# Top-32 attention with routed feed-forward: one copy for the values of two units, a third tile's ranks on ScalarE, and a mask half on GpSimd in six more steps

## The chip, the core and the metric

The kernel runs on one core of a Trainium2 chip. The metric is device time in microseconds (us). Before the change it is 788.99 us, the median of three runs (788.96 to 789.6). One further execution was profiled; all views of the trace below are of it.

A core has five engines that matter here: TensorE (PE in the profile, its weight loads PEld), VectorE (DVE), ScalarE (ACT), GpSimd (POOL) and the queue that issues most DMAs (SP). Each works through its own instructions in program order and waits for the others by semaphores.

## The reference, cut to what matters

```python
# q, k, v: (8 batches, 8 heads, 576, 64);  x: (8, 576, 512) = heads side by side
scores = scale * q @ k.T
kth    = the 32nd largest score of each row
attn   = softmax(where(scores >= kth, scores, -1e9))
x      = attn @ v
# routed feed-forward, per batch
gate   = x @ w_gate                        # one number a token, 576 of them
top    = the 128 tokens with the largest gates
out    = x;  out[top] += sigmoid(gate[top]) * (relu(x[top] @ w1) @ w2)
```

Two selections are made: the 32nd largest of every row of scores (36,864 rows of 576), and the 128 largest of 576 gates in each batch. Only where a token stands among the gates is needed, not a full sort: its rank, that is the number of gates greater than its own, is its slot among the 128 chosen.

## The kernel before

**Units and steps.** The work on scores is cut into 144 units, 18 in each of 8 batches. A unit (L1050) is a tile of 128 rows for two heads; the last tile of a batch has only 64 rows, so there a unit holds four heads, in two halves of 64 partitions. The big loop at L1176 makes one step for each unit and is a software pipeline: step n multiplies the scores of unit n+1, and looks after the units n, n-1, n-2, n-3 and n-4 in later stages. In the order of a unit's life:

1. PE multiplies scores into `ps`; ScalarE copies them to `sc` (`keep`, L530).
2. VectorE finds a lower bound for the 32nd largest: 14 MAX8 over seventh parts (`cand`), then some small rounds that end in `bound` (`find_bound`, L544).
3. ScalarE takes the sign of score against bound and counts it (`part`, L578: `sides`, `seen`).
4. GpSimd multiplies scores by signs into `y` (L1148) and appends eight steps (`fill`, L589).
5. VectorE reads the 32nd largest from `y` with two MAX8 (`find_kth`, L598: `next8`).
6. The mask `less` marks scores below it (`mask`, L603). One head's half is made by ScalarE (Relu), the other by GpSimd (`is_lt`).
7. PE transposes scores and adds the mask into `ptr` (`turn`, L642), and once more into the last 128 columns of the bank `av` (`turn_last`, L662). ScalarE takes the exponential of both (`pT`, `last`).
8. PE multiplies by the values into columns 0 to 129 of `av` (`values`, L674): two heads, each with 64 columns and one for the sum of the weights. ScalarE copies them to `xs` (`keep_values`, L706). The bank `av` has one buffer, taken anew in each step (`room_to_turn`, L632).

All instructions of the loop are kept in the order in which they are written; no scheduler moves them. Within a step ScalarE's order is: `pT` of unit n-4, first `sides` of n-1, `last` of n-4, the mask of n-3, what `flush` gives out from the list `late`, copies of transposed keys and queries, `sc` of n+1, what `flush_copies` gives out, second `sides` of n-1, `xs` of n-4. GpSimd's is: mask of n-3, what `flush_pool` gives out from `pool_late`, `y` of n-1. VectorE's is: `cand` and `bound` of n, with other small work put in among the `cand`, then the 32nd largest of n-2.

**The routed part.** When a batch's x is whole, it is stored, and the steps of the next batch carry the batch's feed-forward as a generator (`mixture`, L770). The tables `mix_at` (L1056) say at which steps its pieces are called: with steps numbered 0 to 17 within the next batch, the start is called at 5, tiles 0 to 4 of the gates at 7, 9, 10, 13 and 14, the places at 16, and the expert's matmuls go on into the batch after. The last but one batch has a denser table (L1062). Tile t's piece does this:

- For t of 0 and 1, `weigh_gates` (L823) runs on ScalarE from `late`, in the step after the call: the sign of each gate in the row less this tile's gate, summed, into `sign_sum`. It writes the 576 signs over `pick`, which is rewritten later. After tile 1, both tiles' slots are picked by GpSimd (`choose_slot`, L807) against `slot_signs`, a row of 575 - 2 x slot.
- For t of 2, 3 and 4, `choose` (L845) runs on VectorE from `vector_late`: a comparison of the 576 gates with this tile's, counted into `rank`. GpSimd then picks against `slot`.

`multiply_places` (L941) turns the picks into row numbers on PE. It writes seven columns of the same bank `av`, behind the values (L868), in the step named in `place_steps`; ScalarE copies them out after `xs`. At the end of the feed-forward GpSimd adds the result rows into the output by an indirect DMA (`add_rows`, L989). In six of the steps in which that DMA is issued (`scatter_steps`, L1074; with batches numbered from 0, step 0 of batches 3 to 7 and step 11 of batch 7), `mask_of` at L1240 gives both halves of the mask to ScalarE.

After the loop there is a tail for the last units and the last batch's routed part. It closes with a test whether all results are sure (from L1528); if not, a general loop repeats everything in a slower way.

Of the kernel before, what the change touches and what calls it, by code (L numbers as in the profile page):

```python
# [12 lines left out]
FP32 = mybir.dt.float32  # L13
BF16 = mybir.dt.bfloat16
FP8 = mybir.dt.float8e4
# [17 lines left out]
J = 4  # L33
# [16 lines left out]
def kernel(  # L50
# [12 lines left out]
    P = nc.NUM_PARTITIONS  # L63
    B, H, S, D = q.shape
# [5 lines left out]
    R = S - JP  # L70
    HALF = S // 2
    DE = D + 1
# [47 lines left out]
    for i in range(2):  # L120
# [37 lines left out]
    nc.gpsimd.memset(ranks, 0.0)  # L158


    signs = const.tile([P, B - 1, 2], FP32, name="signs")
    places = const.tile([P, B, 7], FP32, name="places")
    nc.gpsimd.memset(places, 1.0)
    slot_signs = const.tile([P, CAP], FP32, name="slot_signs")
# [1 line left out]
        out=slot_signs,  # L166
# [234 lines left out]
    def bank(pool, name, **how):  # L401
        return pool.tile([P, 512], FP32, name=name, **how)
# [91 lines left out]
    def heads_of(t, g):  # L494

        if t == J:  # L500
            return [[(4 * g + i, 0), (4 * g + 2 + i, R)] for i in range(2)]
        return [[(2 * g + i, 0)] for i in range(2)]
# [97 lines left out]
        for i in range(2):  # L600
            dve.max(next8[:, i, :], y[:, i, :])

    def mask(sc, next8, on=None):  # L603

        less = wkpool.tile([P, 2, S], BF16, name="less")
        for i, engine in enumerate(on or (act, pool)):
            kth = next8[:, i, 7:8]  # L610
            if engine is act:
                act.activation(less[:, i, :], sc[:, i, :], AF.Relu, bias=kth, scale=-1.0)
            else:

                engine.tensor_scalar(
                    out=less[:, i, :],
                    in0=sc[:, i, :],
                    scalar1=kth,
                    scalar2=None,
                    op0=ALU.is_lt,  # L620
                )
        return less
# [6 lines left out]
                tr, less, out_of_reach, start=False, stop=True, skip_group_check=True  # L629
            )  # L630

    def room_to_turn():  # L632
        return ps_tr.tile([P, 2, J, P], FP32, name="ptr"), ps_av.tile(
            [P, 512], FP32, name="av"
        )


    def by_half(a):
# [32 lines left out]
        turn_some(tr, *last)  # L671
        return tr

    def values(t, g, pT, last, av, vs):  # L674

        vt, vpair = vs
        for i, heads in enumerate(heads_of(t, g)):
            for c in range(J):
                for r in (0, R):
                    h = heads[-1 if r else 0][0]
                    pe.matmul(
                        av[r : r + R, i * DE : (i + 1) * DE],
                        by_half(pT)[:, r // R, i * J + c, :],
                        vt[:, h, c, :],  # L690
                        start=(c == 0 and i == 0),
                        stop=False,
                        skip_group_check=True,
                    )
        for r in (0, R):
            h = heads_of(t, g)[0][-1 if r else 0][0]
            pe.matmul(
                av[r : r + R, 0 : 2 * DE],
                last[:, r : r + R],
                vpair[:, h // 2, :, :].rearrange("p h e -> p (h e)"),  # L700
                start=False,
                stop=True,
                skip_group_check=True,
            )

    def keep_values(t, g, av, xs):  # L706
        n = R if t == J else P
        for h, r in heads_of(t, g)[0]:
            act.copy(
                out=xs[0:n, h : h + 2, :].rearrange("p h e -> p (h e)"),  # L710
                in_=av[r : r + n, 0 : 2 * DE],
            )

    def normalise(b, t, xs):
# [55 lines left out]
    def mixture(row0, pg, rank, exact=False, sign_sum=None):  # L770
# [36 lines left out]
        def choose_slot(t, n, slot=slot, rank=None):  # L807
            if rank is None:
                rank = rank_of[:, t : t + 1]
            pool.tensor_scalar(  # L810
                out=pick[0:n, t, :],
                in0=slot[0:n, :],
                scalar1=rank[0:n, :],
                scalar2=None,
                op0=ALU.is_equal,
            )

        for t in range(NT):
            yield
            n = R if t == J else P  # L820


            def weigh_gates(t=t):  # L823
                total = sign_sum[:, t : t + 1]
                act.activation(
                    pick.rearrange("p t c -> p (t c)")[:, 0:S],
                    gate_row,
                    AF.Sign,
                    bias=gate[:, t : t + 1],
                    scale=-1.0,  # L830
                    accum_out=total,
                )
                if t == 1:
                    for u in range(2):
                        pool_late.append(
                            lambda u=u: choose_slot(
                                u, P, slot_signs, sign_sum[:, u : u + 1]
                            )
                        )

            if t < 2 and not exact:
                late.append(weigh_gates)
                continue

            def choose(t=t, n=n):  # L845
                junk = modpool.tile([P, S], FP32, name="junk", tag="scratch")
                dve.tensor_scalar(
                    out=junk[0:n, :],
                    in0=gate_row[0:n, :],
                    scalar1=gate[0:n, t : t + 1],  # L850
                    scalar2=None,
                    op0=ALU.is_gt,
                    op1=ALU.add,
                    accum_out=rank[0:n, t : t + 1],
                )
                if exact:
                    break_ties(t, gate, gate_row, rank)

                pool_late.append(lambda: choose_slot(t, n))

            vector_late.append(choose)
# [3 lines left out]
            ps = ps_misc.tile([P, 512], FP32, name="place_ps", tag="misc")  # L865
        else:
            ps = values_bank[0]
        ps = ps[:, 2 * DE : 2 * DE + 7]  # L868


        done = B if exact else int(row0) // S + 1
# [198 lines left out]
    for b in range(B - 1):  # L1070
        for i in mix_at_of.get(b, mix_at):
            mix_steps.setdefault((b + 1) * per_batch + i, []).append(b)

    scatter_steps = {  # L1074
        (b + 1) * per_batch + mix_at_of.get(b, mix_at)[-1] + 1 for b in range(B - 2)
    }

    place_steps = {}
    for b in range(B - 1):
        n = (b + 1) * per_batch + mix_at_of.get(b, mix_at)[6]  # L1080
# [86 lines left out]
            out=least[:, b : b + 1], in_=kth, axis=mybir.AxisListType.XY, op=ALU.min  # L1167
        )

    def mask_of(n, on=None):  # L1170
        b, i = divmod(n, per_batch)
        masks[n] = mask(scs[n], next8s[b][:, i, :, :], on)
        if i == per_batch - 1 and b < B - 1:
            keep_least(b, bounds.pop(b)[:, :, :, 7], next8s.pop(b)[:, :, :, 7])

    for n in range(-1, N):  # L1176
# [39 lines left out]


        if is_unit(n - 4):
            tr, av = room_to_turn()
            pT, last, exp, turn_rest = weigh(scs.pop(n - 4), tr, av, masks.pop(n - 4))  # L1220
            exp()
        early = is_unit(n - 1) and n + 1 >= NHP
# [14 lines left out]
        if is_unit(n - 4):  # L1237
            turn_rest()()
        if is_unit(n - 3):
            mask_of(n - 3, (act, act) if n in scatter_steps else None)  # L1240
        flush()
        if is_unit(n + 1) and n + 1 >= NHP:
            b, i = divmod(n, per_batch)
# [19 lines left out]
            sign(n - 1, 1)  # L1263
        if is_unit(n - 4):
            b4, t4, g4 = units[n - 4]
            values(t4, g4, pT, last, av, qkv[b4][2])
            if n in place_steps:
                values_bank[0] = av
                next(mixtures[place_steps[n]])
                pieces[place_steps[n]] += 1  # L1270
            if g4 == 0:
                xs = xpool.tile([P, H, DE], FP32, name="xs")
                if t4 == 0:
                    x = xpool.tile([P, NT, HD], FP32, name="x")
                    pg = gates_of[b4 % 2]
                    of_batch[b4] = x, pg
            keep_values(t4, g4, av, xs)
            if g4 == groups(t4) - 1:
                inverting = b4, t4, xs
                n4 = R if t4 == J else P  # L1280
                keep_sums(n4, xs, sums[0:n4, b4 * NT + t4, :])
            while kept:
                kept.pop(0)()
# [227 lines left out]
    for copy, half, dc in zip((act.copy, dve.tensor_copy), halves, (0, 2)):  # L1511
# [9 lines left out]
        out=low,  # L1521
# [87 lines left out]
    def general_weights(sc):  # L1609

        p = wkpool.tile([P, 2, S], FP32, name="p", tag="y")
        for i in range(2):
            cur, tops = sc[:, i, :], []
            left = wkpool.tile([P, 2, S], FP32, name="left", tag="y")
            for r in range(TOP_K // 8):
                tops.append(stats.tile([P, 8], FP32, name=f"top{r}", bufs=2))
                nc.vector.max(tops[-1], cur)
                if r < TOP_K // 8 - 1:
                    nc.vector.match_replace(left[:, 0, :], tops[-1], cur, LOWEST)
                    cur = left[:, 0, :]  # L1620
            shift = stats.tile([P, 1], FP32, name="shift", bufs=2)
            nc.vector.tensor_scalar_mul(shift, tops[0][:, 0:1], -scale)
            e = wkpool.tile([P, S], FP32, name="e", tag="sides")
            nc.scalar.activation(
                e, sc[:, i, :], AF.Exp, bias=shift, scale=scale
            )
            nc.vector.scalar_tensor_tensor(
                out=p[:, i, :],
                in0=sc[:, i, :],
                scalar=tops[-1][:, 7:8],  # L1630
                in1=e,
                op0=ALU.is_ge,
                op1=ALU.mult,
            )
        return p
# [77 lines left out]
```

## Time and profile before

| what | figure |
|---|---|
| median of three runs | 788.99 us |
| the profiled execution, its own time | 790.52 us |
| its span, first to last instruction | 788.2 us |
| mean granted TensorE clock in it | 0.996 |
| matmuls of scores, `ps` | x1248, 170.5 us |
| values copied, `xs`, 128 partitions | x128, 40.3 us, mean 315 ns |
| values copied, `xs`, 64 partitions | x32, 8.3 us, mean 261 ns |
| gates' signs, `pick` on ScalarE | x14, 11.2 us, and 14 accumulator reads, 3.2 us |
| gates' comparison in the loop, `junk` on VectorE | x21 (14 of 128 partitions, 7 of 64), 16.6 us |
| mask half on GpSimd | x135, 233.8 us, mean 1732 ns |
| mask half on ScalarE | x147, 117.3 us, mean 804 ns |

The profiled execution lasted 790.52 us, 2.3 us more than its span; the median run is 1.5 us shorter than it. Busy time is the union of an engine's instructions. The instructions of one engine overlap at their ends: what one costs the engine is the distance from its start to the next start, not its own length. A copy of 130 columns is listed with 0.27 us or more, and the next instruction starts 0.15 us after it. Sums below use distances between starts, from the timeline, where an engine runs without a break.

### The profile page before, as it was taken

Reading aid. Unit: us, or ns where it says so; the run is one execution under the profiler, and the core shown is the slowest. Engines: PE = TensorE matmul, PEld = TensorE weight load, DVE = VectorE, ACT = ScalarE, POOL = GpSimd, SP = SyncE. Lnnn points to the kernel's source line nnn. Section 1 sums busy time; section 2 is a strip of 40 time slices with the busy share of each in tenths; the row PEclk is TensorE's granted clock in tenths of the full one; section 3 lists DMA queues with packets and bytes.
Section 4 is the critical chain, followed back from the end, with each engine's and each line's share of the span. In section 5 each row is a group of like instructions: output and inputs, shape, how many; then the busy total and the mean of one; then the engine's idle time right before and its main releaser. Section 6 shows DMA issues by size and latency. Waiting matters only on the chain. (4 is left out here: it accounts for less than half of the span.)

```text
span 788.2 us, 33265 instructions
## 1 busy us (share of the span) xinstructions
PE 724.6 (92%) x12535; PEld 550.9 (70%) x12535; DVE 756.7 (96%) x4602; ACT 735.0 (93%) x1612; POOL 698.1 (89%) x732
## 2 busy tenths in 40 slices
PE   8888878788999989999999999999899999999887
PEld 6666666566776668766786667766687668758756
DVE  6999999999999999999999999999999999999952
ACT  5999999999999999999999999999999999989730
POOL 3899999999999999999999999999999999999821
PEclk9999999999999999999999999999999999999899
DMA  8941215121150222321242221412233102101021
GB/s 172 295 86 34 58 63 112 29 56 30 62 113 22 54 68 66 90 50 43 75 94 46 56 43 62 104 30 56 42 96 84 30 16 69 25 16 17 2 75 31
DMA packets 121751, 50.69 MB, mean 64 GB/s; under 512 B 116016, under 2 KB 116016, under 8 KB 120560
## 3 DMA queue, kind: packets, MB, share of 16 engines
q1 hardware_dynamic: 118368, 43.94, 22.4%
q0 software_dynamic: 1744, 4.20, 2.9%
q8 instruction: 101, 1.65, 0.9%
q14 instruction: 66, 0.54, 0.2%
q10 hardware_dynamic: 1472, 0.36, 0.2%
HBM read 36.93 MB, written 11.55 MB: 62 GB/s over the span
## 5 line engine op out<-in xcount | busy, mean ns | idle before, releaser
L46 POOL TENSOR_TENSOR y<-sc,sides 128x576 f32<-128x576 f32 x288 | 350.5, 1234 | 35.7 <-ACT sides L46 33.4
L46 DVE MAX8 cand<-sc 128x8 f32<-128x82 f32 (+1 forms) x2016 | 312.9, 228 | 4.6 <-ACT sc L46 4.6
L46 POOL TENSOR_SCALAR less<-sc,next 128x576 bf16<-128x576 f32 x135 | 233.8, 1732 | 13.0 <-DVE next L46 10.5
L46 ACT ACTIVATE sides<-sc,bound 128x576 fp8e4<-128x576 f32 x288 | 234.3, 814 | 2.1 <-DVE bound L46 2.0
L46 PEld LDWEIGHTS av<-v,pT 128*64 128x64 f32 x4608 | 146.9, 138 | 92.6 <-ACT last L46 81.8
L46 DVE MAX8 next<-y 128x8 f32<-128x584 f32 x288 | 204.4, 751 | 0.0
L46 PE MATMUL av<-v,pT 128*64 128x65 f32 x4608 | 166.9, 225 | 39.6 <-ACT last L46 37.5
L46 PE MATMUL ps<-kT,qT 64*128 64x288 f32 (+1 forms) x1248 | 170.5, 422 | 4.2 <-ACT sc L46 4.2
L46 PEld LDWEIGHTS <-less 64*128 64x128 bf16 (+1 forms) x2448 | 162.4, 132 | 7.7 <-POOL less L46 5.2
L46 ACT COPY sc<-ps 128x1152 f32<-128x1152 f32 x140 | 162.7, 1162 | 0.0
L46 PE MATMUL ptr<-ident,sc 64*128 64x64 f32 x2272 | 158.6, 253 | 0.0
L46 ACT ACTIVATE pT<-ptr 128x1024 f32<-128x1024 f32 x142 | 149.4, 1052 | 8.0 <-PE ptr L46 6.8
L46 PEld LDWEIGHTS ptr<-ident,sc 64*128 64x128 f32 x2272 | 137.7, 137 | 23.8 <-issue 21.2
L46 PE MATMUL ptr<-out_of_reach,less 64*128 64x64 bf16 x2272 | 146.1, 190 | 3.7 <-POOL less L46 3.6
L46 ACT ACTIVATE less<-sc,next 128x576 bf16<-128x576 f32 x147 | 117.3, 804 | 0.0
L46 PEld LDWEIGHTS ps<-kT,qT 64*128 64x128 f32 (+1 forms) x1248 | 92.7, 176 | 23.9 <-ACT sc L46 6.7
L46 DVE MATCH_REPLACE8 cand<-best,cand 128x21 f32<-128x21 f32 (+1 forms) x576 | 98.9, 179 | 0.0
L46 DVE MAX8 best<-cand 128x8 f32<-128x21 f32 (+1 forms) x576 | 90.4, 190 | 0.0
L46 ACT ACTIVATION_READ_ACCUMULATOR sides<-sc,bound 128x1 f32 x288 | 67.4, 234 | 0.0
L46 PE MATMUL h_ps<-xeT,w 128*128 128x128 f32 x464 | 61.9, 278 | 0.0
L46 PEld LDWEIGHTS av<-ident,sc 128*128 128x128 f32 x144 | 20.0, 139 | 55.7 <-issue 27.4
L46 PE MATMUL av<-vpair,last 128*64 128x130 f32 x576 | 56.9, 276 | 0.0
(167 smaller groups left out, 945.5 us busy)
## 6 DMA issues: line engine op xcount, KB each, us to landing
v<-in_v_dram SPq DMA_DIRECT2D x64, 128.0 KB, 3.3
out_dram<-x SPq DMA_DIRECT2D x8, 1024.0 KB, 4.0
rows<-in_k_dram SPq DMA_DIRECT2D x56, 128.0 KB, 2.8
rows<-in_q_dram SPq DMA_DIRECT2D x56, 128.0 KB, 2.9
w<-in_moe_w_dram SPq DMA_DIRECT2D x2, 2048.0 KB, 12.8
gate_row<-row_dram SPq DMA_DIRECT2D x7, 288.0 KB, 3.9
last<-in_q_dram SPq DMA_DIRECT2D x8, 128.0 KB, 3.5
vpair<-in_v_dram SPq DMA_DIRECT2D x16, 64.0 KB, 4.0
```

What stands on the lines that cost most here:

```text
L46: return lambda *a, **kw: self._tc.keep_in_program_order(fn(*a, **kw))
```

## The change

Three edits are made, and a few that they need.

**Values of two units.** `room_to_turn` takes a new bank `av` only for the even unit of a pair; the odd unit goes on in the same tile, and its values are put 130 columns further on (`at`). In the even step nothing is copied. In the odd step one copy of 260 columns takes both (`keep_values_of_two`); in the 64-row tile it is two copies, one for each half of the partitions. The places move from column 130 to column 260 of the bank.

**Ranks of tile 2.** `SIGNED` is 3, so that tile 2 goes to `weigh_gates` on ScalarE instead of `choose` on VectorE. The signs are written to a tile of their own, `gate_signs`, in FP8, and no longer over `pick`. Each tile's slot is picked in the step of its own sum; before, tiles 0 and 1 waited for tile 1.

**Masks.** `scatter_steps` is gone; GpSimd makes its half of the mask in these six steps too.

The tail keeps `keep_values`, one copy a unit. In the general loop, which runs only if a result is unsure, one tile gets another tag.

```diff
-    signs = const.tile([P, B - 1, 2], FP32, name="signs")
+    SIGNED = 3
+    signs = const.tile([P, B - 1, SIGNED], FP32, name="signs")
...
-    def mask(sc, next8, on=None):
+    def mask(sc, next8):
...
-        for i, engine in enumerate(on or (act, pool)):
+        for i, engine in enumerate((act, pool)):
...
-    def room_to_turn():
-        return ps_tr.tile([P, 2, J, P], FP32, name="ptr"), ps_av.tile(
-            [P, 512], FP32, name="av"
-        )
+    def room_to_turn(av=None):
+        tr = ps_tr.tile([P, 2, J, P], FP32, name="ptr")
+        return tr, bank(ps_av, "av") if av is None else av
...
-    def values(t, g, pT, last, av, vs):
+    def values(t, g, pT, last, av, vs, at=0):
...
-                        av[r : r + R, i * DE : (i + 1) * DE],
+                        av[r : r + R, at + i * DE : at + (i + 1) * DE],
...
+    def keep_values_of_two(t, g, av, xs):
+        n = R if t == J else P
+        both = av[:, 0 : 4 * DE]
+        if t < J:
+            act.copy(
+                out=xs[:, 2 * g : 2 * g + 4, :].rearrange("p h e -> p (h e)"), in_=both
+            )
+            return
+        for i, (h, r) in enumerate(heads_of(t, g)[0]):
+            act.copy(
+                out=xs[0:n, :, :].rearrange("p (g i h) e -> p i g (h e)", i=2, h=2)[
+                    :, i, :, :
+                ],
+                in_=both[r : r + n, :].rearrange("p (g c) -> p g c", g=2),
             )
...
             def weigh_gates(t=t):
                 total = sign_sum[:, t : t + 1]
+                unread = modpool.tile([P, S], FP8, name="gate_signs")
                 act.activation(
-                    pick.rearrange("p t c -> p (t c)")[:, 0:S],
+                    unread,
                     gate_row,
                     AF.Sign,
                     bias=gate[:, t : t + 1],
                     scale=-1.0,
                     accum_out=total,
+                    saturate=False,
                 )
-                if t == 1:
-                    for u in range(2):
-                        pool_late.append(
-                            lambda u=u: choose_slot(
-                                u, P, slot_signs, sign_sum[:, u : u + 1]
-                            )
-                        )
-
-            if t < 2 and not exact:
+                pool_late.append(lambda: choose_slot(t, P, slot_signs, total))
+
+            if t < SIGNED and not exact:
                 late.append(weigh_gates)
                 continue
...
-        ps = ps[:, 2 * DE : 2 * DE + 7]
+        ps = ps[:, 4 * DE : 4 * DE + 7]
...
-            tr, av = room_to_turn()
+            second = (n - 4) % 2
+            tr, av = room_to_turn(av if second else None)
...
-            mask_of(n - 3, (act, act) if n in scatter_steps else None)
+            mask_of(n - 3)
...
-            values(t4, g4, pT, last, av, qkv[b4][2])
+            values(t4, g4, pT, last, av, qkv[b4][2], 2 * DE * second)
...
-            keep_values(t4, g4, av, xs)
+            if second:
+                keep_values_of_two(t4, g4 - 1, av, xs)
```

More of the change, by code (lines that the diff above doesn't have):

```diff
@@ L697, in values @@
             pe.matmul(
-                av[r : r + R, 0 : 2 * DE],
+                av[r : r + R, at : at + 2 * DE],
                 last[:, r : r + R],
@@ L711, in keep_values @@
                 in_=av[r : r + n, 0 : 2 * DE],
+            )
[5 more added lines that the diff above has]
+                out=xs[:, 2 * g : 2 * g + 4, :].rearrange("p h e -> p (h e)"), in_=both
+            )
+            return
[5 more added lines that the diff above has]
+                in_=both[r : r + n, :].rearrange("p (g c) -> p g c", g=2),
             )
@@ L1072 @@
             mix_steps.setdefault((b + 1) * per_batch + i, []).append(b)
-    scatter_steps = {
-        (b + 1) * per_batch + mix_at_of.get(b, mix_at)[-1] + 1 for b in range(B - 2)
-    }
     place_steps = {}
@@ L1168, in keep_least, with mask_of @@
         )
-    def mask_of(n, on=None):
+    def mask_of(n):
         b, i = divmod(n, per_batch)
-        masks[n] = mask(scs[n], next8s[b][:, i, :, :], on)
+        masks[n] = mask(scs[n], next8s[b][:, i, :, :])
         if i == per_batch - 1 and b < B - 1:
@@ L1622, in general_weights @@
             nc.vector.tensor_scalar_mul(shift, tops[0][:, 0:1], -scale)
-            e = wkpool.tile([P, S], FP32, name="e", tag="sides")
+            e = modpool.tile([P, S], FP32, name="e", tag="scratch")
             nc.scalar.activation(
```

## The prediction, made before the change was run

> **What bounds the kernel now.** I read the span's slices first, then the busy time of single batches, the waits of VectorE, and last the timelines of one batch.
>
> ```profile
> DVE  6999999999999999999999999999999999999952
> 372.85:465.18 92.33, 88.27 (x1549) 66.57 (x1549) 92.23 (x569) 91.77 (x204) 87.52 (x89) 1.00 0.26 63
> 465.18:557.52 92.34, 88.28 (x1549) 66.58 (x1549) 92.24 (x569) 91.78 (x204) 87.55 (x89) 1.00 0.26 63
> ...
> DVE cand L46 <- ACT sc L46: 4.6, 3, 3.1
> ```
>
> The columns of the two windows are length, PE, PEld, DVE, ACT, POOL (busy us), granted clock, DMA. Batches 4 and 5 take the same time to 0.01 us. VectorE is busy for all but 0.1 us of it, ScalarE for all but 0.6, GpSimd for all but 4.8. The last line is from the waits over 0.15 us (total, times, longest): in all of the span `cand` waited for scores 3 times, at the start, never in these batches. So VectorE sets the pace from about 40 to 740 us (699.2 us busy of 700 in that window), and ScalarE follows so closely that it could take over. What is taken from VectorE there comes off the span as long as its two suppliers, the copy of `sc` (ScalarE) and `y` (GpSimd), stay ahead of it.
>
> **Tile 2's ranks: VectorE's part.** Seven comparisons go, one in step 11 of batches 1 to 6 and one in step 8 of batch 7.
>
> ```profile
> 427.79 1.10 DVE L46 MAX8 cand<-sc 128x8 f32<-128x82 f32 x7
> 428.81 0.80 DVE L46 TENSOR_SCALAR_CACHE_REDUCE junk<-gate_row,gate 128x576 f32<-128x576 f32 x1
> 429.53 0.09 DVE L46 DVE_READ_ACCUMULATOR junk<-gate_row,gate 128x1 f32 x1
> 429.53 1.11 DVE L46 MAX8 cand<-sc 128x8 f32<-128x82 f32 x7
> ```
>
> From start to next start it costs 429.53 - 428.81 = 0.72 us; the accumulator's read lies beside the next MAX8. 7 x 0.72 = **5.0 us** off VectorE, all of it where VectorE is the bound.
>
> **ScalarE's part.** It gets a sign pass for it, in the same step and ahead of the copy of `sc`:
>
> ```profile
> 414.81 0.77 ACT L46 ACTIVATE pick<-gate_row,gate 128x576 bf16<-128x576 f32 x1
> 415.47 0.20 ACT L46 ACTIVATION_READ_ACCUMULATOR pick<-gate_row,gate 128x1 f32 x1
> 415.56 0.36 ACT L46 COPY kT<-ps 128x256 f32<-128x256 f32 x1
> ...
> 417.60 0.27 ACT L46 COPY xs<-av 128x130 f32<-128x130 f32 x1
> 417.75 1.05 ACT L46 ACTIVATE pT<-ptr 128x1024 f32<-128x1024 f32 x1
> ```
>
> 415.56 - 414.81 = 0.75 us more. The FP8 output is not in these rows, but `sides`, FP8 of the same size, has 814 ns a piece against 801 here: no difference.
>
> **Copies of two units.** A copy of 130 columns costs 0.15 (417.60 to 417.75), one of 256 costs 0.26 (415.56 to 415.82), so one of 260 about 0.26 instead of 0.30: 0.04 a pair, 0.3 for the 8 pairs of a batch. In the 64-row tile the timeline has both copies of a unit and what follows at 391.84 and 392.41, 0.57, the other unit 0.55; two copies of 260 are 2 x (0.28 + 130 x 0.11/126) = 0.78, so 0.34 less. Together 0.64 a batch. A rule of the Trainium skill would make much more of it: "ScalarE: Activation LUTs", Rules for kernel authors, budgets about 0.3 us for each activation and 0.83 ns an element. A pair would then go from 0.82 to 0.52, 2.4 us a batch, and ScalarE would be out of the race. The distance of starts gives the same 0.83 to 0.87 ns an element but only some 0.04 us a piece, as the rest overlaps the next instruction; I take the row.
>
> In even steps the next `pT` comes up 0.15 earlier and may have to wait for PE's `ptr`; where it does already (three steps of 18, about 0.6 us a batch), that share is not won. In odd steps `turn_last` no longer waits for the copy, a small gain for PE.
>
> **Masks.** In five step 0s and in step 11 of batch 7 ScalarE loses a mask half: 0.67 (414.14 to 414.81 in its timeline). GpSimd gains 1.72:
>
> ```profile
> 373.59 1.60 POOL L46 DMA_INDIRECT out_dram<-gy,row_i  x1 [0.17 <-ACT less L46]
> 374.68 2.92 POOL L46 TENSOR_TENSOR y<-sc,sides 128x576 f32<-128x576 f32 x2
> 377.55 0.23 POOL L46 TENSOR_TENSOR y<-steps,seen 128x16 f32<-128x16 f32 x1
> 377.88 1.73 POOL L46 TENSOR_SCALAR less<-sc,next 128x576 bf16<-128x576 f32 x1
> 379.58 1.21 POOL L46 TENSOR_TENSOR y<-sc,sides 128x576 f32<-128x576 f32 x1
> 381.84 1.22 POOL L46 TENSOR_TENSOR y<-sc,sides 128x576 f32<-128x576 f32 x1 [1.05 <-ACT sides L46]
> ```
>
> The added mask stands ahead of the indirect DMA at 373.59 and is over at about 375.1. Behind it come the DMA, this step's `y` and the next mask. The pair of `y` at 374.68 hides some 0.5 us of waiting (2.92 against 2.4) and the next one 1.05, so GpSimd has caught up after two steps. On the way its `y` is 1.1 late; VectorE reads it about 2.8 after it is written. The mask is late for PE's transposes of step 1 (they end at 375.4 now) by perhaps 0.3, which takes some of ScalarE's 0.67. The indirect DMA starts 1.7 later and lands 4.9 after issue, 5 us ahead of SP's store of the next x at 385.96, the first in SP's queue that could meet it. In step 11 of batch 7 VectorE's own lead is over 3 us.
>
> **ScalarE's sum** for a batch with all parts: + 0.75 - 0.64 - 0.67 = -0.56. In batches 1 and 2 there is no mask: +0.11, where the scores lie over 1.6 us ahead. Is `sc` still in time? At its tightest, step 11, the copy (426.21, 1.20 long) ends at 427.41 and `cand` starts at 427.79: 0.38 ahead. One step later it is 433.26 - (430.89 + 1.24) = 1.13. The masks, the 64-row copies and four pairs lie before it, 1.15 gained, perhaps 0.8 after what PE holds back; step 11 takes 0.75 + 0.72 again. So 1.1 at step 11 and 1.13 + 0.8 - 1.47 = 0.5 at step 12: thin, yet no wait.
>
> **GpSimd's picks.** Tile 0's pick (0.6) moves from step 10 to step 8, where `y` waits 0.4 for `sides` anyway; tile 2's waits for ScalarE now, whose sum is there about when the mask before it ends. Nothing on the path.
>
> **The lock.** VectorE's gate products (`prod`, five a batch) read two tensors. They cost 0.60 free (419.01 to 419.61), but more beside GpSimd:
>
> ```profile
> 388.95 0.78 DVE L46 CUSTOM_DVE_ANT_0 prod<-x,wg 128x512 f32<-128x512 f32 x1
> 388.45 1.72 POOL L46 TENSOR_SCALAR less<-sc,next 128x576 bf16<-128x576 f32 x1
> 439.38 1.03 DVE L46 CUSTOM_DVE_ANT_0 prod<-x,wg 128x512 f32<-128x512 f32 x1
> 437.44 2.41 POOL L46 TENSOR_TENSOR y<-sc,sides 128x576 f32<-128x576 f32 x2
> ```
>
> The second waited for `y` to end at 439.85: +0.35. The first met a mask that ran on to 390.17 and yet was held only 0.11. The Trainium skill, "SBUF — State Buffer", Who interferes with whom, says that whoever is first keeps the shared ports for the whole instruction. That speaks against masks for GpSimd: up to 1.2 us here, 1.7 at worst. By the row a mask holds them for its first 0.6 us only, so six more masks, none in a step with a `prod` but its neighbours shifted, cost 0 to 0.6 each: at most 3.6 by the row, 10 by the rule. But `y` does hold to its end. This batch's five products lose 0.63; a new phase between the engines can take that away (-4.4 us in seven batches) or bring more. I take no difference.
>
> **Sum.** The profiled span 788.2 - 5.0 = 783.2. Its execution was 1.5 above the median run, so for the median: 788.99 - 5.0 = **784.0**.
>
> **Rivals.**
>
> - *VectorE stays the bound* (0.64): 782 to 785.5.
> - *ScalarE or PE takes over* (0.14). For: ScalarE has 0.6 of 92.3 free and loses only 0.56, part of which PE holds back; the new sign pass stands ahead of the tightest copy. Against: 0.5 remains by the sum above. Then a batch falls by 0.3 to 0.4: 2.5, 786.5.
> - *Nothing is won* (0.10): what VectorE frees in step 11 returns as a wait for `sc` in step 12, 0.72 each time: 789. The profile's periodic batches speak against it, since ScalarE regains 2.7 us of lead by step 17.
> - *Slower through the lock* (0.10): VectorE's product of step 13 comes 0.7 earlier against `y` or another falls on a `y` just begun. One product a batch behind a whole `y` is 1.2, 8.4 in seven, 3.4 net: 792.4. It decides from an average of 0.72 more waiting a batch.
> - *It does not do what it says* (0.02): tile 2's sums are wrong, the closing test sees places that don't add up to one, and the general loop runs over all batches, some hundreds of us more.
>
> Range: 782 less some of the lock's gain, 781.5, up to no change, 788.5. What a measurement here can tell from no change is 0.2%, 1.6 us: faster 0.77, same 0.11, slower 0.12.
>
> **What would show it.** A batch of 91.6 us instead of 92.33, VectorE busy throughout; step 11 at 4.75 instead of 5.47; no new wait of `cand` for `sc`; `xs` with 260 columns at 0.37 to 0.42. I am wrong if VectorE waits for `sc` at steps 12 and 13, if `prod` is longer on average than now (0.82 for 128 rows), or if PE's transposes wait for GpSimd's mask at step 1 for more than 0.7 us.

## The result, and the profile after

The changed kernel takes 791.06 us, the median of 12 runs (790.5 to 796.02), against 789.31 us for the kernel before on the same chip (12 runs, 788.94 to 790.38). The ratio is 1.0028, 95% interval 1.0017 to 1.004: slower by about 2 us, where 5 us less had been forecast.

In the profiled executions the difference seems smaller: 791.04 us after (span 788.5) against 790.52 (span 788.2). The start of the program hides what the loop lost. The first `cand` of unit 2 starts at 15.51 us in the profile after and at 17.44 in the one before; over all kernels below this start lies between 15.1 and 17.6 without regard to what was edited. From that `cand` to the one of unit 143 it is 724.77 us after and 720.58 before: 4.2 more. So the loop is compared from here on, batch by batch.

Here are the window of batch 4 (length, then PE, PEld, DVE, ACT, POOL busy, clock, DMA share, GB/s) and the line of VectorE's waits for scores, both of the kernel after:

```profile
369.98:462.42 92.44, 88.29 (x1549) 66.75 (x1549) 92.28 (x566) 91.09 (x195) 89.02 (x90) 1.00 0.26 63
...
DVE cand L46 <- ACT sc L46: 2.9, 3, 2.1
```

VectorE is as full as before (92.28 of 92.44). ScalarE has become emptier, 91.09 against 91.77, by 0.68 where 0.56 was forecast, and GpSimd fuller by 1.5. Yet a batch lasts 0.11 longer, and VectorE has a comparison less to do in it. An engine that is as busy with less to do has instructions that became longer. Where, the distances between the first `cand` of one step and of the next tell (batch 4, the steps that differ by over 0.1):

| step | before | after | what is in it |
|---|---|---|---|
| 3 | 5.70 | 6.15 | `prod` of tile 3 |
| 5 | 5.53 | 5.37 | `prod` of tile 4 |
| 11 | 5.47 | 4.74 | tile 2's comparison, gone |
| 12 | 4.81 | 4.96 | a wait for `sc` at its end |
| 13 | 5.70 | 6.10 | `prod` of tile 1 |

Step 11 gives the 0.73 us that were forecast. The two products take them back. Here they are in the timeline of the kernel after, each with the GpSimd instruction beside it (start, length):

```profile
386.08 1.22 DVE L46 CUSTOM_DVE_ANT_0 prod<-x,wg 128x512 f32<-128x512 f32 x1
385.93 1.80 POOL L46 TENSOR_SCALAR less<-sc,next 128x576 bf16<-128x576 f32 x1
436.21 1.43 DVE L46 CUSTOM_DVE_ANT_0 prod<-x,wg 128x512 f32<-128x512 f32 x1
434.70 2.40 POOL L46 TENSOR_TENSOR y<-sc,sides 128x576 f32<-128x576 f32 x2
```

The first product was shown before with a mask that had begun 0.50 earlier, and took 0.78; now the mask is only 0.15 old. The second met a `y` with 0.47 still to run; now 0.89 is left (434.70 + 2.40 - 436.21).

The mask of step 3 is later because GpSimd has not caught up with the mask that was added in step 0. From the indirect DMA at 372.44 it works without a pause into step 3, and its first wait is at 389.14; in the kernel before it had waited 1.05 as early as 381.84. Two of its lines in that stretch:

```profile
376.14 2.22 POOL L46 TENSOR_SCALAR less<-sc,next 128x576 bf16<-128x576 f32 x1
...
389.14 1.21 POOL L46 TENSOR_TENSOR y<-sc,sides 128x576 f32<-128x576 f32 x1 [0.23 <-ACT sides L46]
```

Batch 7 is worse: 4.8 us longer up to step 17, nearly all of it one product.

```profile
717.08 5.55 DVE L46 CUSTOM_DVE_ANT_0 prod<-x,wg 128x512 f32<-128x512 f32 x1
...
708.63 1.62 POOL L46 DMA_INDIRECT out_dram<-gy,row_i  x1 [0.18 <-issue]
709.76 2.92 POOL L46 TENSOR_TENSOR y<-sc,sides 128x576 f32<-128x576 f32 x2
712.10 0.75 POOL L46 TENSOR_TENSOR y<-steps,seen 128x16 f32<-128x16 f32 x1
712.29 2.26 POOL L46 TENSOR_SCALAR less<-sc,next 128x576 bf16<-128x576 f32 x1
713.99 1.56 POOL L46 TENSOR_TENSOR x<-xs,rden 128x512 f32<-128x512 f32 x1
714.99 2.89 POOL L46 TENSOR_TENSOR y<-sc,sides 128x576 f32<-128x576 f32 x2
717.35 0.70 POOL L46 TENSOR_TENSOR y<-steps,seen 128x16 f32<-128x16 f32 x1
717.55 2.19 POOL L46 TENSOR_SCALAR less<-sc,next 128x576 bf16<-128x576 f32 x1
719.24 2.84 POOL L46 TENSOR_TENSOR y<-sc,sides 128x576 f32<-128x576 f32 x2
721.57 1.12 POOL L46 TENSOR_TENSOR y<-steps,seen 128x16 f32<-128x16 f32 x1
726.28 1.72 POOL L46 TENSOR_SCALAR less<-sc,next 128x576 bf16<-128x576 f32 x1 [3.59 <-DVE next L46]
```

This product took 0.68 in the kernel before. Look at the GpSimd lines: from the indirect DMA on, each instruction starts some 0.5 us before the one ahead of it ends (712.10 against 709.76 + 2.92 = 712.68, and so on). The product comes out at 722.6, only when GpSimd has nothing left to run.

All 32 products of 128 rows are 9.7 us longer in sum (mean 1.13 against 0.82), those of 64 rows 0.6 shorter. That is 9.1 lost, less 5.2 from the seven steps without the comparison (6 x 0.73 + 0.86), plus some 0.6 for scores (four times 0.15): 4.5, beside the 4.2 measured in the loop.

### The profile page after: what moved, and what is told of

Read it like the earlier page. It is cut to its first block, busy times and chain, and to the rows that moved or that the text cites. A ratio compares the mean times of both kernels' runs of the same rounds, so it can differ in the third digit from the quotient of the medians.

```text
span 788.5 us, 33168 instructions
## 1 busy us (share of the span) xinstructions
PE 724.0 (92%) x12535; PEld 550.4 (70%) x12535; DVE 760.9 (97%) x4588; ACT 730.9 (93%) x1543; POOL 708.6 (90%) x738
## 3 DMA queue, kind: packets, MB, share of 16 engines
q8 instruction: 101, 1.65, 0.9%
## 5 line engine op out<-in xcount | busy, mean ns | idle before, releaser
L46 POOL TENSOR_SCALAR less<-sc,next 128x576 bf16<-128x576 f32 x141 | 248.1, 1759 | 17.6 <-DVE next L46 13.5
L46 ACT ACTIVATE sides<-sc,bound 128x576 fp8e4<-128x576 f32 x288 | 231.2, 803 | 3.3 <-DVE bound L46 3.3
L46 ACT ACTIVATE pT<-ptr 128x1024 f32<-128x1024 f32 x142 | 147.3, 1038 | 15.1 <-PE ptr L46 14.6
L46 ACT COPY sc<-ps 128x1152 f32<-128x1152 f32 x140 | 160.9, 1149 | 0.0
L46 PE MATMUL ptr<-ident,sc 64*128 64x64 f32 x2272 | 160.5, 253 | 0.0
L46 ACT ACTIVATE less<-sc,next 128x576 bf16<-128x576 f32 x141 | 111.8, 793 | 0.0
L46 ACT ACTIVATION_READ_ACCUMULATOR sides<-sc,bound 128x1 f32 x288 | 64.4, 224 | 0.0
```

The source lines that it names most:

```text
L46: return lambda *a, **kw: self._tc.keep_in_program_order(fn(*a, **kw))
```

## The experiments

Two theories were held against each other. **A, the lock**: products that wait for GpSimd eat the gain. **B, supply**: ScalarE or TensorE has become the pace-maker. "Batch 4" is the distance from the first `cand` of that batch to the first of the next, "batch 7" from its step 0 to its step 17, both from the one profiled execution.

| kernel | median, us | ratio to before, interval | batch 4 | batch 7 |
|---|---|---|---|---|
| before | | 1 | 92.33 | 88.18 |
| after | 791.06 | 1.0028, 1.0017 to 1.004 | 92.44 | 92.98 |
| x1_masks_back | 785.82 | 0.9966, 0.995 to 0.9981 | 92.25 | 87.63 |
| x2_only_masks | 795.18 | 1.0084, 1.0062 to 1.0106 | 92.97 | 93.38 |
| x3_only_ranks | 789.15 | 1.0000, 0.9986 to 1.0014 | 92.74 | 87.68 |
| x4_only_copies | 787.79 | 0.9990, 0.9975 to 1.0005 | 92.35 | 87.80 |
| x5_one_mask_back | 786.08 | 0.9985, 0.9974 to 0.9996 | 92.11 | 88.12 |
| x6_before_one_input | 783.94 | 0.9954, 0.994 to 0.9967 | 91.96 | 87.06 |
| x7_after_one_input | 778.98 | 0.9895, 0.988 to 0.9911 | 91.53 | 86.19 |
| x8_moved_products | 781.68 | 0.9930, 0.9917 to 0.9944 | 92.17 | 86.75 |
| x9_moved_three | 791.81 | 1.0019, 1.0009 to 1.003 | 92.54 | 89.51 |
| x10_moved_all_masks | 796.44 | 1.0076, 1.0059 to 1.0092 | 93.50 | 89.95 |
| x11_no_scatter | 788.73 | 0.9984, 0.9974 to 0.9994 | 92.59 | 88.94 |
| x12_one_input_masks_back | 782.80 | 0.9920, 0.9902 to 0.9939 | 92.25 | 86.85 |

The kernel before had medians of 789.31, 788.34 (x1 to x4), 787.68 (x5 to x8), 789.94 (x9 to x11) and 789.30 (x12) beside them, so ratios are compared.

### The edits one by one

**x1_masks_back**: the changed kernel, with both halves of the mask on ScalarE again in the six steps.

```diff
-            mask_of(n - 3)
+            mask_of(n - 3, (act, act) if n in scatter_steps else None)
```

> The changed kernel with the mask edit alone undone: in the six steps ScalarE makes both halves again; ranks and copies stay changed. Theory A (lock: the late GpSimd queue keeps VectorE's two-input gate products waiting): the 5.55 us product in batch 7 and the 1.22 us products in step 3 of batches 3 to 7 go back to about 0.7 to 0.8, about 7 us come off: 784 us, ratio to before 0.993 to 0.995. Theory B (supply: ScalarE has become the pace-maker, cand waits for sc): ScalarE gets 6 x 0.67 us more and the kernel is slower than the changed one, 791 to 795.

It is faster than the kernel before, but by 0.34%, where A expected 0.5 to 0.7%. In batch 7 the product of step 13 takes 0.67 again. In batch 4 the products of steps 3 and 13 still take 0.92 and 1.42, and step 12 has a wait for scores of 0.25. A was not enough for this kernel; x12 below shows what else holds it.

**x2_only_masks**: the kernel before, with the masks' edit alone.

```diff
-            mask_of(n - 3, (act, act) if n in scatter_steps else None)
+            mask_of(n - 3)
```

> The kernel before with the mask edit alone. Theory A: the long product in batch 7 (about 5 us) and some 0.45 us at step 3 of five batches come without anything in return: 792 to 796, ratio 1.004 to 1.009. Theory B: ScalarE is relieved of 4 us, VectorE is the bound: 788 to 789.5, no change.

```profile
387.67 1.22 DVE L46 CUSTOM_DVE_ANT_0 prod<-x,wg 128x512 f32<-128x512 f32 x1
...
720.77 5.53 DVE L46 CUSTOM_DVE_ANT_0 prod<-x,wg 128x512 f32<-128x512 f32 x1
```

With nothing else changed, this edit costs 0.84%, and the timeline has the same two marks: the product of step 3 at 1.22, that of step 13 of batch 7 at 5.53. Scores are further ahead than in the kernel before (1.9 us at step 12 against 1.1). So a kernel whose ScalarE was relieved became slower, which B can't explain. Nor is it GpSimd as a supplier: VectorE was never idle before `next`, its reading of `y`, in this kernel as in the changed one (0.0 us in both).

**x3_only_ranks**: the kernel before with tile 2's ranks on ScalarE, signs in their own tile, nothing else.

```diff
+    SIGNED = 3
...
-            if t < 2 and not exact:
+            if t < SIGNED and not exact:
...
```

> The kernel before with tile 2's ranks on ScalarE alone (and the tile tag that this needs). VectorE loses 7 x 0.72 = 5.0 us. Theory A: step 13's product then waits longer for y (1.4 instead of 1.03, some 2 us in all), the rest is won: 786 to 787. Theory B: without the relief of ScalarE cand waits for sc at step 12 by about 0.4 a batch besides: 788 to 790.

Here both theories have a part. The comparison is gone, but the batch is longer, 92.74: the product of step 13 takes 1.53, and VectorE now waits for scores at the ends of steps 11 and 12 (5.08 and 4.97 between starts, against 4.74 and 4.81 where nothing is waited for), 0.5 together. The line of the waits of this kernel, beside the 3 times of the kernel before:

```profile
DVE cand L46 <- ACT sc L46: 4.0, 7, 2.1
```

**x4_only_copies**: the kernel before with one copy for the values of two units alone.

```diff
-            keep_values(t4, g4, av, xs)
+            if second:
+                keep_values_of_two(t4, g4 - 1, av, xs)
```

> The kernel before with the copies of two units alone. VectorE's work is unchanged. Both theories: within 1 us of before, 788.3 to 790.3; by A any difference is in the length of the gate products, by B it is faster if ScalarE or PE had a part in the pace.

No difference that can be measured: what this saves is ScalarE's, and by itself ScalarE was not the bound.

**x5_one_mask_back**: the changed kernel, with one single mask on ScalarE again, that of step 11 of batch 7.

```diff
-            mask_of(n - 3)
+            mask_of(n - 3, (act, act) if n == 137 else None)
```

> The changed kernel with one of the six masks given back to ScalarE, that of step 11 in batch 7 (n = 137). Theory A: the queue of GpSimd drains before step 13 of that batch, its product takes about 0.7 instead of 5.55 us, the rest stays: 4.9 us less than the changed kernel, ratio to before 0.996 to 0.998. Theory B: ScalarE gets 0.67 us more, nothing else: as the changed kernel or slower, 1.002 to 1.004.

```profile
715.61 0.67 DVE L46 CUSTOM_DVE_ANT_0 prod<-x,wg 128x512 f32<-128x512 f32 x1
```

One mask of 1.7 us decides over 4.9 us: the product is back at 0.67, and the ratio goes from 1.0028 to 0.9985. The two kernels have the same instructions up to that step, yet batch 4 lasts 92.11 here and 92.44 in the profile of the changed kernel. Some 0.3 us a batch thus comes from how the engines happen to stand to one another in an execution, and no difference of that size between two profiles is given a cause here unless its rows show one.

### The lock taken out

**x6_before_one_input** and **x7_after_one_input**: in both kernels the product reads one tensor and one number a row, instead of two tensors. The gates become sums of x scaled by one weight a row.

```diff
-        dve.tensor_tensor_reduce(
+        dve.tensor_scalar(
...
-            in1=wg[0:n, :],
-            scale=1.0,
-            scalar=0.0,
+            scalar1=wg[0:n, 0:1],
+            scalar2=None,
```

> The kernel before, the gate products replaced by a scaled sum of x over its columns with accumulation, which reads one tensor: the gates are other numbers, so other tokens are routed; all else is done as before. Theory A: the waits of the products go (0.6 us a batch, 1.3 in batch 7): 783 to 785, ratio 0.992 to 0.995. Theory B: products never mattered: 788 to 789.

> The changed kernel with the same replacement (gates are sums of x). Theory A: all that the change lost in the products is gone, and the 5.0 us of tile 2 appear, less what cand then waits for sc at steps 12 and 13 (0.2 to 0.4 a batch): 2 to 4.5 us less than the kernel before with the replacement, some 779 to 782, ratio to before 0.988 to 0.992. Theory B: the change remains slower than the kernel before with the replacement, by 1 to 3 us.

The view of all products of x7 (shortest, median, longest in ns), and the window of its batch 5:

```profile
L46 DVE TENSOR_SCALAR_CACHE_REDUCE prod<-x,wg x40: 719/727/745, 50.1 to 746.2; 128x512 f32<-128x512 f32 x32, 64x512 f32<-64x512 f32 x8
...
458.56:550.11 91.55, 88.03 (x1549) 66.65 (x1549) 91.29 (x567) 91.03 (x195) 88.20 (x90) 1.00 0.26 63
```

Nothing holds these products: 0.72 to 0.75 at all 40 places, whatever GpSimd does. Now the change brings most of what was forecast. From x6 to x7 the median falls from 783.94 to 778.98, 5.0 us. That this is 7 x 0.72 to a tenth is partly chance: the medians are of 5 and 4 runs, and in the profiled executions the loop is 4.2 shorter, by 0.7 to 0.9 in batches 1, 2, 3 and 7 but by only 0.4 in batches 4 to 6. Only the products (and with them the tokens that are routed) differ between the pair of kernels whose time went up 1.8 us and the pair whose time went down 5.0. So the lost gain is the products' waiting, as A says. What is missing in batches 4 to 6 goes to ScalarE: scores come only 0.03 to 0.06 ahead at steps 12 and 13, and steps 11 and 12 last 4.78 and 5.08 where 4.74 and 4.81 are enough, 0.3 together.

**x12_one_input_masks_back**: x7, with the masks of the six steps on ScalarE again (the edit of x1).

> The changed kernel with one-input gate products (as in x7, the routed tokens are others) and with the masks of the six steps back on ScalarE: are these masks worth anything once no VectorE product can be held? In x7 the scores come only 0.03 to 0.06 us ahead at steps 12 and 13, so ScalarE paces there. If ScalarE's relief counts, each of the five batches with a mask in step 0 pays up to 0.67 us as waits for scores at steps 12 and 13: 1.5 to 3.4 us above x7, a ratio of 0.9915 to 0.994 and a batch of 91.8 to 92.2. If the relief is lost in ScalarE's waits for TensorE and VectorE, nothing: 0.9885 to 0.9905, a batch of 91.5.

This tells what the masks are worth to ScalarE. The windows of x12 and then of x1:

```profile
460.08:552.34 92.26, 88.33 (x1550) 66.90 (x1549) 91.42 (x567) 91.76 (x196) 86.71 (x89) 1.00 0.26 63
```

```profile
369.40:461.65 92.25, 88.34 (x1555) 66.72 (x1553) 92.01 (x566) 91.75 (x196) 87.64 (x89) 1.00 0.26 63
```

With the masks on ScalarE a batch lasts 92.25, whether products are held (x1) or never are (x12). ScalarE has the same 91.75 in both; only VectorE's busy time differs, 92.01 against 91.42, since an instruction that is held counts as busy. So in x1's batches 3 to 6 ScalarE sets the pace, and the products' waiting costs nothing: VectorE would wait for scores instead. That is why x1 gained less than A expected. And moving the masks to GpSimd is worth 0.7 us a batch (92.26 - 91.55) as long as no product is held for it.

### Other places for the products

A product is held by what GpSimd has just begun, so it might be put elsewhere. So far a product stands behind the second `cand` of its step's second head.

**x8_moved_products**: masks of the six steps on ScalarE; tile 1's product (and tile 0's in batch 7) behind `bound`, tile 3's two `cand` later. `u` is the place among the seven `cand`, 99 is behind `bound`.

```diff
-            amid_late.append(lambda a=gating: gates(*a))
+            amid_late.append(
+                (
+                    99 if gating[1] == 1 or gating == (B - 1, 0) else 4 if gating[1] == 3 else 2,
+                    lambda a=gating: gates(*a),
+                )
+            )
```

> The changed kernel with the masks on ScalarE in the six steps, and two of the five gate products of a batch moved within their step to where GpSimd is inside a mask: tile 1's (and tile 0's in batch 7) behind the bound, tile 3's two cand later. Theory A: against the same without the move (0.9966 of before) 0.7 us a batch at step 13, 0.25 at step 3 and 1.6 in batch 7 go, some of it comes back as waits for sc: 779 to 782, ratio 0.989 to 0.993. Theory B: the place of the products is of no account, ratio 0.996 to 0.997.

This is the fastest version that leaves nothing out: 0.9930, 781.68 us, ahead of both kernels. Tile 3's product and the mask beside it in x8:

```profile
384.63 0.68 DVE L46 CUSTOM_DVE_ANT_0 prod<-x,wg 128x512 f32<-128x512 f32 x1
...
384.69 2.21 POOL L46 TENSOR_SCALAR less<-sc,next 128x576 bf16<-128x576 f32 x1
```

Here the product comes 0.06 us ahead of the mask, and it is the mask that waits: 2.21 instead of 1.72. In the changed kernel it came 0.15 behind, and took 1.22. Tile 0's product, which was left where it was, now falls on a `y` and takes 1.39 (0.67 in the changed kernel). That was no loss, for ScalarE paces these batches at 92.17, as in x12. What x8 gains over x1 therefore lies elsewhere: 0.6 to 0.9 us in each of batches 1, 2 and 7, and less than 0.1 in each of batches 3 to 6, where A had expected 0.7 too.

**x9_moved_three**: x8, with tile 0's product moved behind `bound` in every batch, to gain that 0.7 too.

```diff
-                    99 if gating[1] == 1 or gating == (B - 1, 0) else 4 if gating[1] == 3 else 2,
+                    99 if gating[1] in (0, 1) else 4 if gating[1] == 3 else 2,
```

> The last kernel (masks on ScalarE, products of tiles 1 and 3 moved; 0.993 of before) with tile 0's product behind the bound in every batch, since its trace shows that one at 1.40 us behind a whole y. Theory A: 0.7 us a batch less until ScalarE's own 91.5 us a batch are the bound: 778 to 780, ratio 0.988 to 0.991. Theory B: no change from 0.993.

```profile
515.42 1.59 DVE L46 CUSTOM_DVE_ANT_0 prod<-x,wg 128x512 f32<-128x512 f32 x1
...
515.24 2.85 POOL L46 TENSOR_TENSOR y<-sc,sides 128x576 f32<-128x576 f32 x2
```

A miss. The moved product falls on a `y` that is 0.18 old. With VectorE later, ScalarE and GpSimd are further ahead (scores 1.3 us at step 9 against 0.03 in x8), and `y` comes where the product had been put to avoid it. Tile 1's takes 1.30 in turn, and in batch 7 tile 0's 3.49, from 702.10 through the end of a mask and two `y` (702.64 to 705.03).

**x10_moved_all_masks**: the changed kernel with its masks, tiles 0 and 1 behind `bound`, tile 3 four `cand` later.

```diff
...
+                    99 if gating[1] in (0, 1) else 6 if gating[1] == 3 else 2,
...
```

> The changed kernel with all its masks on GpSimd, and the products of tiles 0, 1 and 3 moved away from y and the start of a mask. Theory A: if the masks harm only through the products, the moved products at steps 3, 9 and 13 take about 0.7, and what remains is the one in batch 7 behind GpSimd's full queue, 3 us or less: 778 to 782, ratio 0.988 to 0.993. Theory B: the masks stay slower than before, over 1.0.

A second miss, and with x2 the slowest: the products take 1.6 at step 9, 1.8 at step 13, 1.1 at step 5, 4.55 in batch 7. A place in the program is not a place beside GpSimd: every edit moves the phases of both engines.

### The product of 5.55 us

**x11_no_scatter**: the changed kernel; the indirect DMA of step 11 of batch 7 is replaced by an addition of two inputs on GpSimd.

```diff
+        if not exact and int(row0) // S == B - 3:
+            late.append(
+                lambda: pool_late.append(lambda: pool.tensor_tensor(gy, gy, gy, ALU.add))
+            )
+            return
```

> The changed kernel with the indirect DMA behind the added mask of batch 7 (step 11) replaced by a two-input addition of about the same length on GpSimd: the expert's rows of one batch are not added to the output. If it is only GpSimd's lateness that keeps the product of step 13 waiting, that product takes 4 us or more again and the time stays 1.002 to 1.004 of before. If it is the state after the indirect DMA, in which each GpSimd instruction starts before the one ahead has ended, the product takes at most 1.5 us: 4 us less, 0.996 to 0.999.

```profile
717.77 1.43 DVE L46 CUSTOM_DVE_ANT_0 prod<-x,wg 128x512 f32<-128x512 f32 x1
...
709.14 1.03 POOL L46 TENSOR_TENSOR gy<-gy 128x512 f32<-128x512 f32 x1
710.14 2.38 POOL L46 TENSOR_TENSOR y<-sc,sides 128x576 f32<-128x576 f32 x2
712.48 0.21 POOL L46 TENSOR_TENSOR y<-steps,seen 128x16 f32<-128x16 f32 x1
712.68 1.72 POOL L46 TENSOR_SCALAR less<-sc,next 128x576 bf16<-128x576 f32 x1
```

The mask of step 11 stands where it stands in the changed kernel (0.76 us after the step's first `cand`, there 0.75), but the instructions behind it have their usual length and follow one another without that overlap, and the product takes 1.43. With the DMA and without the mask (x5) it takes 0.67; with both, 5.55. In this place the 5 us come only with both.

That the overlap is what keeps the product waiting is argued, not shown. The addition took 1.03 us and the DMA 1.62, so in x11 GpSimd is 0.8 less late, and the product comes as a `y` ends instead of 0.81 before. That difference alone may be worth some 0.8, an estimate from the product of step 9 in batch 7 of the changed kernel: it met an ordinary `y` with the same 0.81 left and took 2.25. So over 3 of the 5.55 us remain for the overlap. But in x9 a product waited 3.49 where no instructions overlapped, so long waits have another way to come about. Why a waiting product gets no turn stays open.

## Why the prediction was wrong

**Right: the bound and the gain.** VectorE set the pace, and a comparison was worth 0.72: step 11 fell by 0.73. With nothing holding the products (x6 to x7) the change gave 5.0 by the medians and 4.2 by the profiled loops.

**Right: ScalarE's sum, not quite its lead.** Forecast -0.56 a batch, -0.68 in the windows. The 0.3 us for each activation of "ScalarE: Activation LUTs" (the Trainium skill, Rules for kernel authors), weighed there against the row's 0.04, would have relieved ScalarE by some 1.8 us more; the windows side with the row. (The 0.3 is stated for an ACTIVATE with its bias in a column of its own; these copies are another instruction.) The lead of the scores was taken too well: 0.15 us at step 12 instead of 0.5. ScalarE's waits for TensorE's transposes (`pT` for `ptr`, those over 0.15) rose from 0.2 to 1.1 us in batch 4, so the relief did not become lead. A wait of 0.15 for scores follows one step on. The rival "ScalarE or PE takes over" thus had a part of 0.15 a batch in the changed kernel, and ScalarE paced batches 3 to 6 in x1 and x12.

**Wrong: the lock, at "I take no difference".** The paragraph had the mechanism and priced its bounds, and then put nothing into the sum. That is the term that failed: taken as 0, it measured 9.1 us. The five products that lost 0.63 in the batch shown lose 1.3 in the changed kernel's batch 4 (0.56 for tile 3, 0.76 for tile 1, almost nothing for the rest), and one in batch 7 alone loses 4.9. Over the loop the products take 9.1 us more than before, 1.3 a batch on average, past the 0.72 from which the rival "slower through the lock" was said to decide. It gave 792.4; 791.06 came. That the two are so close is partly luck: the rival had reckoned with one product a batch behind a whole `y`, 8.4 in all. What came was 2.7 at step 13 of batches 1 to 6, 2.4 at step 3 and 4.9 in a single product of batch 7, less some 0.8 elsewhere.

The same account fits the other kernels. In x2 the products are 7.95 us longer in sum, and its loop is 7.8 longer. In x9 and x10 they are 9.2 and 13.4 longer; less the 5.2 of the comparison that is 4.0 and 8.2, and the loops are 3.9 and 8.1 longer. In x1, x3 and x8 the loop is 0.9, 2.3 and 2.3 longer than this account gives, about what VectorE waits for scores there. The runs split the loss by the parts of the change, since the products of steps 3 and 13 of batch 5 differ from kernel to kernel (us):

| kernel | masks on GpSimd | ranks on ScalarE | step 3 | step 13 |
|---|---|---|---|---|
| before | no | no | 0.79 | 1.02 |
| x4_only_copies | no | no | 0.67 | 1.03 |
| x2_only_masks | yes | no | 1.26 | 1.11 |
| x3_only_ranks | no | yes | 0.89 | 1.54 |
| x1_masks_back | no | yes | 0.93 | 1.42 |
| after | yes | yes | 1.26 | 1.43 |

- *Step 13 goes with the ranks*, 1.42 to 1.54 against 1.02 to 1.11. With 0.73 less in step 11, the product meets the same `y` earlier: 0.89 of it was left instead of 0.47. The rival had named this shift at 0.7; 0.42 came. (In x2 and x4 the product meets a mask there, 0.17 and 0.25 old, and not a `y`.) As the shift follows from the gain itself, it belonged in the main sum.
- *Step 3 goes with the masks*, 1.26 against 0.67 to 0.93. The forecast had "0 to 0.6 each" for neighbours that are shifted. It took none of that into the sum, since GpSimd "has caught up after two steps". That was wrong: in the changed kernel it works without a pause into step 3, and in batch 4 the mask of step 3 came 0.36 later against the product. The forecast's own figures fell short, 0.5 + 1.05 of waiting against a mask of 1.72. And the 0.5 was no waiting: the DMA ahead ended at 375.19 (373.59 + 1.60), and the two `y` were over 2.41 later, the usual length of a pair. In batches 1 and 2 of the changed kernel, where no mask was added, the product of step 3 takes 0.68.
- *Batch 7* is the masks' too: x2 has it, x1 and x5 don't. The forecast had looked at step 11 for VectorE's lead over `y` alone, not for the product behind it. The fill ahead of that product's mask ended 0.68 before the product started in the kernel before, and 0.97 after it in the changed kernel: GpSimd stands 1.65 later, nearly the whole added mask. The forecast's bound by the rule of the Trainium skill (1.7 at worst for a mask) lies far under 4.9.

That rule ("SBUF — State Buffer", Who interferes with whom) also says that a VectorE instruction with at most one SBUF input doesn't contend, outside of the modes with two ports, and that the order of issue decides who blocks. x6 and x7 agree with the first (0.72 to 0.75 in all places), the pair of lines of x8 with the second. The lock for the whole instruction holds for `y`, but a mask mostly held a product for its first 0.6 to 0.7 us only, as the row had said; the exceptions are the waits of 3.49 to 5.55 in batch 7.

**The signs named beforehand.** Step 11 at 4.75 came (4.74); a batch of 91.6 came only in x7 (91.53). Of the three that would tell of a wrong forecast, the mean of `prod` above 0.82 (1.13) was the one that spoke at once. The wait for scores came too, but with 0.15 at one step. TensorE's waits for GpSimd's masks rose to 6.1 from 3.6 us; those of step 1 were 0.4 to 0.6, under the 0.7 named.

## What to carry to other kernels

Before a shared port is left out of a sum as "no difference", take every instruction of the bound engine that can be held there, write down how old its opponent is when it starts, and shift that by what the change takes away ahead of it. An instruction with one tensor input wasn't held anywhere, so where a sum can be had in that form it is a better repair than another place in the program, whose phase each further edit moves. (Here that form computes other gates, so it was an experiment only.) And judge an edit that relieves a supplier together with the one that needs it: the ranks alone gave nothing and the masks alone cost 0.84%, yet with the lock out of the way the whole change gave 4 to 5 us.

## What was not expected of the hardware

After the indirect DMA of step 11 in batch 7, GpSimd's instructions are shown some 0.5 us longer, each starting 0.5 before the one ahead ends, until GpSimd runs out of work. From start to start they are no slower: two `y` are 1.17 apart, as elsewhere. The same is seen in batches 3 to 7 behind the indirect DMA of step 0 wherever a mask was added there, as in the line at 376.14 (2.22 instead of 1.72). Where GpSimd has to wait soon after the DMA, as in the kernel before, it ends with the first `y`.

A VectorE product of two tensors stood through 4.9 us of such a stretch. The stretch alone does not do it. In x2 the products of step 3 in batches 3 to 7 come within 0.05 of the end of a fill in such a stretch, ahead of a mask, and take 1.21 to 1.26; in x10 one that comes 0.03 behind such a fill takes 4.55.

Elsewhere a product that comes up during a `y` gets its turn as `y` ends, and the fill behind it then takes 0.68 instead of 0.21. In step 9 of batch 7, though (2.25 us in the changed kernel, 2.00 in the one before), the fill and the first 0.6 to 0.7 us of a mask passed ahead of it, and in x9 two whole `y`. What decides between the two stays open.
